# Load order, a weight transposed by DMA, and the first FFN units in token halves: one change to a fused attention and FFN kernel

## The chip, the cores and the metric

The kernel runs on one core of a Trainium2 chip, in one launch. The metric is the device time in microseconds (us), the median of the runs shown; the profile is one execution of its own, with every time counted from the start of its span. PE is the matrix engine (TensorE), DVE is VectorE, ACT is ScalarE, POOL is GpSimd, SP is SyncE, which here only issues DMAs.

## The reference

Two branches work on the same layer-normalised input and are added to it. Everything is bfloat16 in memory; B is 1, S is 2048 tokens, D is 512, there are 32 heads of 16, and F is 1792.

```python
xn = layernorm(A_x)
# branch A: linear attention with a softmax feature map
q, k, v = split(xn @ A_wqkv)                          # heads of 16
pq, pk = q @ w_phi[h], k @ w_phi[h]                   # 16x16 for each head
phi(p) = concat(softmax(p), softmax(-p))              # over the 16 features
kv, z = sum_s phi(pk) v, sum_s phi(pk)
o = (phi(pq) @ kv) / (phi(pq) . z + 1e-6)
# branch B: a bilinear gated FFN
y = ((xn @ w_gate) * (xn @ w_up)) @ w_down
out = A_x + o @ A_wo + y
```

## The kernel before

**Tiles.** Tokens go in 16 tiles of 128 (`n`), and four tiles make a group `T` of 512. `xall` holds x with tokens on the partitions, `xnT` the normalised x transposed, so that D lies on the partitions in four chunks `c`. Token p of tile n is row 16p + n of x: a load of several tiles finds their rows side by side.

**Weights folded.** q and k are never formed. `make_bd` (L212) spreads `w_phi` into a block diagonal `bd`, and `fold` (L225) multiplies it with the transposed wq or wk (`wT2`), which gives `W1q` and `W1k`, four 128x512 blocks in two calls of two blocks each. `features` (L238) then is one projection, two exponentials, a sum, a reciprocal and a product. wk is transposed on PE (`wk_transposes`, L217, two blocks of eight 128x128 transposes, each followed by a ScalarE copy of 128x1024), wq by a transposing DMA (L379) in the middle of the kernel.

**LayerNorm.** The first four tiles go one by one: DVE takes the statistics (L146), aggregates them, adds epsilon, POOL raises to -0.5 (L157), DVE scales (L162), PE transposes (`lt`, L207), ACT copies into `xnT` (L208). DVE runs its instructions in the order in which the code emits them; the statistics of tile n+1 stand ahead of the scaling of tile n. Later groups (`ln_block`) are cut into "chores" that are called between other work; their transposes are DMAs issued on SP.

**FFN.** A unit is one pair (T, f): four matmuls of gate and four of up into two PSUM banks, a ScalarE copy of the gate product (L279), and a DVE product (L280) into `hT`. `ffn(k)` (L263) does the next k units of a list of 56; `fin` (L282) forms the output of a tile from 14 chunks of `hT` and 4 of the attention result.

**Order.** The order on every engine is the order of the code. All matmul results share one pool of six PSUM banks in turn. The first part, and what follows it:

```python
lt(0)
warm_up(2)
vproj(0, amid=lambda: lt(1))
vproj(1, copy=nc.vector.tensor_copy, amid=lambda: lt(2))
wk_transposes(0)
vproj(2, copy=nc.vector.tensor_copy, amid=lambda: lt(3))
wk_transposes(1)
vproj(3, copy=nc.vector.tensor_copy)
ffn(1); fold(1, W1k, (0, 1)); ffn(1); fold(1, W1k, (2, 3)); ffn(1)
```

`vproj(n)` (L310) is four matmuls with wv; after the first two it lets the next tile's transposes in. Ahead of all this PE runs ten warm-up matmuls on zeros. After it come `ln_block(4)`, the k projections of tiles 0 to 3 with units between them, then a loop over tiles 4 to 15 (v, k, unit, kv, unit), and last the attention and `fin` of all tiles with the units that are left.

**Loads.** All loads are issued at the start. SP issues x in pieces (tile 0, tile 1, tiles 2 and 3), wk, the first 256 columns of gate and up, w_phi, columns 256 to 895 of both, x of tiles 4 to 7, the remaining columns, x of tiles 8 to 15, w_down and wo, in that order (L76 to L89). ScalarE issues wv (L97) right after its first activation.

Of the kernel before, what the change touches and what calls it, by code (L numbers as in the profile page):

```python
# [8 lines left out]
BF16 = mybir.dt.bfloat16  # L9
F32 = mybir.dt.float32  # L10
AF = mybir.ActivationFunctionType
ALU = mybir.AluOpType
# [9 lines left out]
def kernel(  # L22
# [12 lines left out]
    nc = tc.nc  # L35
    P = 128
    S, D = A_x.shape[-2], A_x.shape[-1]
    F = B_w_gate.shape[-1]
    H = 32
    DH = D // H  # L40
    NT = S // P
# [5 lines left out]
    TT = GT * P  # L47
    E1 = DH + 1

    x_view = A_x.flatten_outer_dims().rearrange("(p n) d -> p n d", n=NT)  # L50
    out_view = out.flatten_outer_dims().rearrange("(p n) d -> p n d", n=NT)

    consts = ctx.enter_context(tc.tile_pool(name="consts", bufs=1))
    wpool = ctx.enter_context(tc.tile_pool(name="wpool", bufs=1))
# [8 lines left out]
    wo = wpool.tile([P, DC, D], BF16)  # L63

    hpool = ctx.enter_context(tc.tile_pool(name="hpool", bufs=3))
    wk = hpool.tile([P, DC, D], BF16, name="wk", tag="h")
    wT2 = hpool.tile([P, 2, DC, D], BF16, name="wT2", tag="h")

    def dma_x(lo, hi):
        nc.sync.dma_start(out=xall[:, lo:hi, :], in_=x_view[:, lo:hi, :])  # L70

    def dma_cols(eng, w, src, lo, hi, at=0):
        eng.dma_start(out=w[:, :, lo - at:hi - at], in_=src[:, lo:hi].rearrange("(c p) f -> p c f", p=P))

    F1, F2 = 2 * P, 7 * P
    for lo, hi in ((0, 1), (1, 2), (2, 4)):  # L76
        dma_x(lo, hi)
    dma_cols(nc.sync, wk, A_wqkv, D, 2 * D, at=D)
    dma_cols(nc.sync, wg, B_w_gate, 0, F1)
    dma_cols(nc.sync, wu, B_w_up, 0, F1)  # L80
    nc.sync.dma_start(out=wphi[:], in_=A_w_phi.rearrange("(c h) d f -> (h d) c f", c=DC))
    dma_cols(nc.sync, wg, B_w_gate, F1, F2)
    dma_cols(nc.sync, wu, B_w_up, F1, F2)
    dma_x(4, 8)
    dma_cols(nc.sync, wg, B_w_gate, F2, F)
    dma_cols(nc.sync, wu, B_w_up, F2, F)
    dma_x(8, NT)
    nc.sync.dma_start(out=wd[:], in_=B_w_down.rearrange("(c p) d -> p c d", p=P))
    nc.sync.dma_start(out=wo[:], in_=A_wo.rearrange("(c p) n -> p c n", p=P))  # L89
# [4 lines left out]
    nc.vector.memset(zeros[:], 0.0)  # L94
    first = consts.tile([P, 1], BF16)
    nc.scalar.activation(out=first[:], in_=zeros[:, 0:1], func=AF.Exp, scale=1.0)
    dma_cols(nc.scalar, wv, A_wqkv, 2 * D, 3 * D, at=2 * D)  # L97
    ident = consts.tile([P, P], BF16)
    make_identity(nc, ident[:])
    mhalf = consts.tile([P, GT], F32)  # L100
# [38 lines left out]
    def bank(name, dt=F32, n=TT):  # L139
        return ps_s.tile([P, n], dt, name=name, tag="s")  # L140
# [9 lines left out]
        stats = ln_sums(n)  # L150
        nc.vector.bn_aggr(out=mv, in_=stats[:])

    def ln_rstd(mv, k):
        ve = lnpool.tile([P, GT], F32, name="ve")
        nc.vector.tensor_scalar(out=ve[:, 0:k], in0=mv[:, 0:k, 1], scalar1=EPS, scalar2=None, op0=ALU.add)
        rstd = lnpool.tile([P, GT], F32, name="rstd", bufs=GT)
        nc.gpsimd.tensor_tensor(out=rstd[:, 0:k], in0=ve[:, 0:k], in1=mhalf[:, 0:k], op=ALU.pow)  # L157
        return rstd
# [18 lines left out]
    def ln_block(lo):  # L177
        mv = mv_tile()
        nb = lnpool.tile([P, GT], F32, name="nb", bufs=GT)
        rstd = []  # L180

        def scales():
            ve = lnpool.tile([P, GT], F32, name="ve4")
            nc.gpsimd.tensor_scalar(out=ve[:], in0=mv[:, :, 1], scalar1=EPS, scalar2=None, op0=ALU.add)
            r = lnpool.tile([P, GT], F32, name="rstd4", bufs=GT)
            nc.gpsimd.tensor_tensor(out=r[:], in0=ve[:], in1=mhalf[:], op=ALU.pow)
            nm = lnpool.tile([P, GT], F32, name="nm")
            nc.gpsimd.tensor_scalar(out=nm[:], in0=mv[:, :, 0], scalar1=-1.0, scalar2=None, op0=ALU.mult)
            nc.gpsimd.tensor_tensor(out=nb[:], in0=nm[:], in1=r[:], op=ALU.mult)
            rstd.append(r)  # L190

        def apply(i):
            xn = xnpool.tile([P, D], BF16, name="xn")
            nc.scalar.activation(out=xn[:], in_=xall[:, lo + i, :], func=AF.Identity,
                                 scale=rstd[0][:, i:i + 1], bias=nb[:, i:i + 1])
            nc.sync.dma_start(out=xnT[:, :, (lo + i) * P:(lo + i + 1) * P], in_=xn[:], transpose=True)

        for i in range(GT):
            chores.append(lambda i=i: ln_stats(lo + i, mv[:, i, :]))
        chores.append(scales)  # L200
        for i in range(GT):
            chores.append(lambda i=i: apply(i))

    def lt(n):
        tp = bank("tp", BF16).rearrange("p (c t) -> p c t", c=DC)
        for c in range(DC):
            nc.tensor.transpose(out=tp[:, c, :], in_=xns[n][:, c * P:(c + 1) * P], identity=ident[:])  # L207
        nc.scalar.copy(out=xnT[:, :, n * P:(n + 1) * P], in_=tp)  # L208

    bd = consts.tile([P, DC, 8, DH], BF16)  # L210

    def make_bd():  # L212
        bo, wp = BO[:], wphi[:]
        nc.gpsimd.tensor_tensor(out=bd[:], in0=_bcast_ap(bo, [bo.ap[0], [0, DC], [E1, 8], [1, DH]]),
                                in1=_bcast_ap(wp, [wp.ap[0], [DH, DC], [0, 8], [1, DH]]), op=ALU.mult)

    def wk_transposes(jp):  # L217
        tp = bank("tp", BF16, 2 * TT).rearrange("p (c t) -> p c t", c=DC)
        for i in range(2):
            j = jp * 2 + i  # L220
            for c in range(DC):
                nc.tensor.transpose(out=tp[:, c, i * P:(i + 1) * P], in_=wk[:, j, c * P:(c + 1) * P], identity=ident[:])  # L222
        nc.scalar.copy(out=wT2[:, 1, :, jp * 2 * P:(jp + 1) * 2 * P], in_=tp)

    def fold(qk, dst, js, copy=nc.scalar.copy):  # L225
        for j in js:
# [33 lines left out]
    hTs = {}  # L260
    units = [(T, f) for T in range(NGRP) for f in range(FC)]

    def ffn(k):  # L263
        for _ in range(k):
            if not units:
                return
            T, f = units.pop(0)
            if f == 0:
                hTs[T] = hpool.tile([P, FC, TT], BF16, name="hT", tag="h")
            gps = bank("g")  # L270
            for c in range(DC):
                nc.tensor.matmul(gps, lhsT=wg[:, c, f * P:(f + 1) * P], rhs=xnT[:, c, T * TT:(T + 1) * TT],  # L272
                                 start=(c == 0), stop=(c == DC - 1))
            ups = bank("u")
            for c in range(DC):
                nc.tensor.matmul(ups, lhsT=wu[:, c, f * P:(f + 1) * P], rhs=xnT[:, c, T * TT:(T + 1) * TT],  # L276
                                 start=(c == 0), stop=(c == DC - 1))
            g_sb = gpool.tile([P, TT], BF16, name="g_sb")
            nc.scalar.copy(out=g_sb[:], in_=gps)  # L279
            nc.vector.tensor_tensor(out=hTs[T][:, f, :], in0=ups, in1=g_sb[:], op=ALU.mult)  # L280

    def fin(n, parts=1):  # L282
        T, t4 = n // GT, n % GT
        w = D // parts
        for lo in range(0, D, w):
            ps = bank("fin")[:, 0:w]
            for f in range(FC):
                nc.tensor.matmul(ps, lhsT=hTs[T][:, f, t4 * P:(t4 + 1) * P], rhs=wd[:, f, lo:lo + w],  # L288
                                 start=(f == 0), stop=False)
            for c in range(DC):  # L290
                nc.tensor.matmul(ps, lhsT=oTs[n][:, c, :], rhs=wo[:, c, lo:lo + w],  # L291
                                 start=False, stop=(c == DC - 1))
            o_sb = opool.tile([P, w], BF16, name=f"o_sb{w}")
            nc.vector.tensor_tensor(out=o_sb[:], in0=ps, in1=xall[:, n, lo:lo + w], op=ALU.add)  # L294
            nc.sync.dma_start(out=out_view[:, n, lo:lo + w], in_=o_sb[:])


    warm = bank("warm")
# [1 line left out]
    def warm_up(k):  # L300
        for _ in range(k):
            nc.tensor.matmul(warm, lhsT=zeros[:, 0:P], rhs=zeros[:], start=True, stop=True)
# [3 lines left out]
    with tc.tile_pool(name="ps_k", bufs=1, space=PSUM) as ps_k:  # L306
# [3 lines left out]
        def vproj(n, copy=nc.scalar.copy, amid=None):  # L310
            ps = bank("pv")
            proj(ps, n, wv, range(2))
            if amid is not None:
                amid()
            proj(ps, n, wv, range(2, DC))
            copy(out=vts[n % NV][:, :, :, 0:DH], in_=ps.rearrange("p (a b c) -> p a b c", a=8, b=4))  # L316
# [17 lines left out]
        for n in range(GT):  # L334
            stats = ln_sums(n)
            if n > 0:
                first_apply(n - 1)
            nc.vector.bn_aggr(out=mvs[n][:, 0, :], in_=stats[:])
            rstds.append(ln_rstd(mvs[n], 1))
        first_apply(GT - 1)  # L340
        make_bd()
        nc.gpsimd.tensor_tensor(out=M4[:], in0=BO[:, 0:4, :], in1=BO[:, 4:8, :], op=ALU.add)
        lt(0)
        warm_up(2)
        vproj(0, amid=lambda: lt(1))
        vproj(1, copy=nc.vector.tensor_copy, amid=lambda: lt(2))
        wk_transposes(0)
        vproj(2, copy=nc.vector.tensor_copy, amid=lambda: lt(3))
        wk_transposes(1)
        vproj(3, copy=nc.vector.tensor_copy)  # L350
        ffn(1)
        fold(1, W1k, (0, 1))
        ffn(1)
        fold(1, W1k, (2, 3))
        ffn(1)
        ln_block(4)
        ffn(1)
        chore(2)
# [16 lines left out]
        chore()  # L375
        ffn(1)
        kv(1)
        ffn(1)
        nc.sync.dma_start(out=wT2[:, 0, :, :], in_=A_wqkv[:, 0:D], transpose=True)  # L379
        for n in range(GT, NT):  # L380
            if n in (4, 8):
# [87 lines left out]
```

## Time and profile before

| | |
|---|---|
| median of 3 runs | 225.45 us (225.12 to 225.52) |
| the profiled execution | 224.9 us, of which its span is 223.2 us |
| PE busy | 217.4 us, 97% of the span |
| DVE, ACT, POOL busy | 137.9, 90.3, 72.1 us |
| read from HBM, written | 9.19 MB, 2.10 MB |

The page divides the span into 40 slices of 5.6 us and gives for each the busy share of an engine in tenths. The chain of waits follows the work that ended last back to the start; a piece of it gives its start, its duration, the engine and the line. A duration of a matmul includes the drain of its pipeline, so that four matmuls of 512 columns in a row show 0.86 us when others follow, and about 0.17 more when PE waits after them. For a DMA the view gives the time of issue and the time from there to its landing.

### The profile page before, as it was taken

Reading aid. Unit: us, or ns where it says so; the run is one execution under the profiler, and the core shown is the slowest. Engines: PE = TensorE matmul, PEld = TensorE weight load, DVE = VectorE, ACT = ScalarE, POOL = GpSimd, SP = SyncE. Lnnn points to the kernel's source line nnn. Section 1 sums busy time; section 2 is a strip of 40 time slices with the busy share of each in tenths; the row PEclk is TensorE's granted clock in tenths of the full one; section 3 lists DMA queues with packets and bytes.
Section 4 is the critical chain, followed back from the end, with each engine's and each line's share of the span. In section 5 each row is a group of like instructions: output and inputs, shape, how many; then the busy total and the mean of one; then the engine's idle time right before and its main releaser. Section 6 shows DMA issues by size and latency. Waiting matters only on the chain.

```text
span 223.2 us, 3437 instructions
## 1 busy us (share of the span) xinstructions
PE 217.4 (97%) x1278; PEld 105.4 (47%) x1278; DVE 137.9 (62%) x237; ACT 90.3 (40%) x161; POOL 72.1 (32%) x59
## 2 busy tenths in 40 slices
PE   7799999999999999999999999999999999999994
PEld 2354444445444444444454444444444444444453
DVE  5634986586559875757679975097745746444321
ACT  2574575448955685646354122222222222100000
POOL 3310455336235663636315453014033033000000
PEclk9999999999999999999999999999999999999999
DMA  6999923501110224020203664314431431622301
GB/s 178 317 381 394 349 55 74 94 1 21 38 38 0 47 50 94 1 47 3 47 1 71 99 140 94 75 24 94 94 73 24 93 72 24 91 55 71 72 25 47
DMA packets 44481, 19.91 MB, mean 89 GB/s; under 512 B 35248, under 2 KB 44080, under 8 KB 44336
## 3 DMA queue, kind: packets, MB, share of 16 engines
q1 hardware_dynamic: 43936, 19.16, 34.8%
q10 hardware_dynamic: 528, 0.52, 0.8%
q8 instruction: 10, 0.16, 0.3%
q14 instruction: 7, 0.06, 0.1%
HBM read 9.19 MB, written 2.10 MB: 51 GB/s over the span
## 4 chain that ended last, share of the span: by engine, by line
PE 95%; DMA 2%; DVE 1%; SPq 0%; ACT 0%; issue 0%
PE fin L288 22%; PE u L276 22%; PE g L272 22%; PE fin L291 6%; PE k L235 6%; PE q L235 6%; PE pv L235 6%; DMA xall<-in_A_x_dram 2%; PE ab L412 2%; PE kv L324 2%; PE pq L229 1%; PE tp L222 0%; PE tp L207 0%; SPq L70 0%; DVE stats L146 0%; ACT xnT L208 0%
## 5 line engine op out<-in xcount | busy, mean ns | idle before, releaser
L276 PE MATMUL u<-xnT,wu 128*128 128x512 bf16 x224 | 57.5, 379 | 0.0
L272 PE MATMUL g<-xnT,wg 128*128 128x512 bf16 x224 | 57.5, 379 | 0.0
L280 DVE TENSOR_TENSOR hT<-u,g_sb 128x512 bf16<-128x512 f32 x56 | 37.1, 668 | 28.3 <-PE u L276 19.5
L247 DVE TENSOR_REDUCE sums<-e 128x64 f32<-128x1024 f32 x32 | 38.9, 1215 | 21.5 <-ACT e L244 21.5
L279 ACT CAST g_sb<-g 128x512 bf16<-128x512 f32 x56 | 32.9, 588 | 46.5 <-PE g L272 46.5
L288 PE MATMUL fin<-wd,hT 128*128 128x512 bf16 (+1 forms) x238 | 51.1, 366 | 0.0
L251 POOL TENSOR_TENSOR phiq<-e,rs 128x1024 bf16<-128x1024 f32 x16 | 30.9, 1932 | 61.5 <-DVE rs L249 53.2
L251 POOL TENSOR_TENSOR phik<-e,rs 128x1024 bf16<-128x1024 f32 x16 | 30.9, 1932 | 47.6 <-DVE rs L249 45.6
L276 PEld LDWEIGHTS <-wu 128*128 128x128 bf16 x224 | 21.9, 98 | 26.4
L288 PEld LDWEIGHTS <-hT 128*128 128x128 bf16 x238 | 23.0, 98 | 24.1
L272 PEld LDWEIGHTS <-wg 128*128 128x128 bf16 x224 | 21.1, 98 | 23.4
L235 PEld LDWEIGHTS <-xnT 128*128 128x128 bf16 x192 | 17.2, 97 | 18.7 <-ACT xnT L208 1.7
L294 DVE TENSOR_TENSOR o_sb<-fin,xall 128x512 bf16<-128x512 f32 (+1 forms) x17 | 11.2, 656 | 22.4 <-PE fin L291 22.4
L243 ACT ACTIVATE e<-q 128x512 f32<-128x512 f32 x16 | 9.5, 596 | 26.1 <-PE q L235 26.1
L249 DVE RECIPROCAL rs<-sums 128x64 f32<-128x64 f32 x32 | 17.7, 553 | 3.1
L235 PE MATMUL pv<-wv,xnT 128*128 128x512 bf16 x64 | 16.9, 379 | 0.6 <-ACT xnT L208 0.5
L291 PE MATMUL fin<-wo,oT 128*128 128x512 bf16 (+1 forms) x68 | 16.6, 366 | 0.0
L235 PE MATMUL k<-W1k,xnT 128*128 128x512 bf16 x64 | 16.4, 379 | 0.0
L235 PE MATMUL q<-W1q,xnT 128*128 128x512 bf16 x64 | 16.4, 378 | 0.0
L243 ACT ACTIVATE e<-k 128x512 f32<-128x512 f32 x16 | 9.6, 597 | 7.0 <-PE k L235 7.0
L316 ACT CAST vt<-pv 128x512 bf16<-128x512 f32 x13 | 7.7, 591 | 11.5 <-PE pv L235 11.5
L146 DVE BATCH_NORM_STATS2 stats<-xall 128x6 f32<-128x512 bf16 x16 | 10.7, 670 | 2.2 <-DMA xall<-in_A_x_dram 2.2
(50 smaller groups left out, 125.1 us busy)
## 6 DMA issues: line engine op xcount, KB each, us to landing
out_dram<-o_sb SPq DMA_DIRECT2D x15, 128.0 KB, 1.9
wd<-in_B_w_down_dram SPq DMA_DIRECT2D x1, 1792.0 KB, 17.5
xall<-in_A_x_dram SPq DMA_DIRECT2D x1, 1024.0 KB, 13.4
wg<-in_B_w_gate_dram SPq DMA_DIRECT2D x1, 896.0 KB, 8.5
wu<-in_B_w_up_dram SPq DMA_DIRECT2D x1, 896.0 KB, 11.4
wg<-in_B_w_gate_dram SPq DMA_DIRECT2D x1, 640.0 KB, 7.9
wu<-in_B_w_up_dram SPq DMA_DIRECT2D x1, 640.0 KB, 7.0
wv<-in_A_wqkv_dram ACTq DMA_DIRECT2D x1, 512.0 KB, 4.4
```

The costliest lines, as they stand in the source:

```text
L235: nc.tensor.matmul(ps, lhsT=xnT[:, j, n * P:(n + 1) * P], rhs=w[:, j, :], start=(j == 0), stop=(j == DC - 1))
L243: nc.scalar.activation(out=e[:, :, 0, :], in_=pfv, func=AF.Exp, scale=1.0)
L247: nc.vector.tensor_reduce(out=sums[:], in_=ev, axis=AX.X, op=ALU.add)
L249: nc.vector.reciprocal(out=rs[:].rearrange("p a b -> p (a b)"), in_=sums[:])
L251: nc.gpsimd.tensor_tensor(out=phi[:].rearrange("p g (x f) -> p (g x) f", f=DH), in0=ev, in1=rs[:].to_broadcast((P, 2 * H, DH)), op=ALU.mult)
L272: nc.tensor.matmul(gps, lhsT=wg[:, c, f * P:(f + 1) * P], rhs=xnT[:, c, T * TT:(T + 1) * TT], start=(c == 0), stop=(c == DC - 1))
L276: nc.tensor.matmul(ups, lhsT=wu[:, c, f * P:(f + 1) * P], rhs=xnT[:, c, T * TT:(T + 1) * TT], start=(c == 0), stop=(c == DC - 1))
L279: nc.scalar.copy(out=g_sb[:], in_=gps)
L280: nc.vector.tensor_tensor(out=hTs[T][:, f, :], in0=ups, in1=g_sb[:], op=ALU.mult)
L288: nc.tensor.matmul(ps, lhsT=hTs[T][:, f, t4 * P:(t4 + 1) * P], rhs=wd[:, f, lo:lo + w], start=(f == 0), stop=False)
L291: nc.tensor.matmul(ps, lhsT=oTs[n][:, c, :], rhs=wo[:, c, lo:lo + w], start=False, stop=(c == DC - 1))
L294: nc.vector.tensor_tensor(out=o_sb[:], in0=ps, in1=xall[:, n, lo:lo + w], op=ALU.add)
```

## The change

The loads are all issued on SP, in a new order: x of tile 0, tile 1, tiles 2 and 3, then wv, the first 256 columns of gate and up, w_phi, columns 256 to 511, then wk as a transposing DMA from DRAM straight into `wT2`, columns 512 to 1151, x of tiles 4 to 7, and the rest. wk's plain load, its sixteen PE transposes and their two copies are gone. Token p of tile n in the first group is now row 128n + p; the other twelve tiles have rows 512 + 12p + (n - 4). The copies of the first two transposed tiles are made in two halves, one warm-up fewer is run, v1's copy goes from DVE to ScalarE, and the first two FFN units are done for tokens 0 to 255 between the v projections and for tokens 256 to 511 after them. One unit that stood before `vproj(4)` now comes ahead of the first k projection. `ln_rstd` takes the engine as an argument, with the same instructions on the same engines as before.

```diff
-    x_view = A_x.flatten_outer_dims().rearrange("(p n) d -> p n d", n=NT)
-    out_view = out.flatten_outer_dims().rearrange("(p n) d -> p n d", n=NT)
+    def token_views(ap):
+        rows = ap.flatten_outer_dims()
+        first = rows[0:TT, :].rearrange("(n p) d -> p n d", p=P)
+        rest = rows[TT:S, :].rearrange("(p n) d -> p n d", p=P)
+        return lambda lo, hi: first[:, lo:hi, :] if hi <= GT else rest[:, lo - GT:hi - GT, :]
...
-    F1, F2 = 2 * P, 7 * P
-    for lo, hi in ((0, 1), (1, 2), (2, 4)):
-        dma_x(lo, hi)
-    dma_cols(nc.sync, wk, A_wqkv, D, 2 * D, at=D)
-    dma_cols(nc.sync, wg, B_w_gate, 0, F1)
-    dma_cols(nc.sync, wu, B_w_up, 0, F1)
+    def dma_gu(lo, hi):
+        dma_cols(nc.sync, wg, B_w_gate, lo * P, hi * P)
+        dma_cols(nc.sync, wu, B_w_up, lo * P, hi * P)
+
+    dma_x(0, 1)
+    dma_x(1, 2)
+    dma_x(2, 4)
+    dma_cols(nc.sync, wv, A_wqkv, 2 * D, 3 * D, at=2 * D)
+    dma_gu(0, 2)
     nc.sync.dma_start(out=wphi[:], in_=A_w_phi.rearrange("(c h) d f -> (h d) c f", c=DC))
-    dma_cols(nc.sync, wg, B_w_gate, F1, F2)
-    dma_cols(nc.sync, wu, B_w_up, F1, F2)
+    dma_gu(2, 4)
+    nc.sync.dma_start(out=wT2[:, 1, :, :], in_=A_wqkv[:, D:2 * D], transpose=True)
+    dma_gu(4, 9)
     dma_x(4, 8)
-    dma_cols(nc.sync, wg, B_w_gate, F2, F)
-    dma_cols(nc.sync, wu, B_w_up, F2, F)
+    dma_gu(9, FC)
     dma_x(8, NT)
...
-    dma_cols(nc.scalar, wv, A_wqkv, 2 * D, 3 * D, at=2 * D)
...
-    def lt(n):
+    def lt(n, parts=1):
...
-        nc.scalar.copy(out=xnT[:, :, n * P:(n + 1) * P], in_=tp)
+        for c in range(0, DC, DC // parts):
+            nc.scalar.copy(out=xnT[:, c:c + DC // parts, n * P:(n + 1) * P], in_=tp[:, c:c + DC // parts, :])
...
-    def wk_transposes(jp):
...
+    def unit(T, f, lo=0, hi=TT):
+        if T not in hTs:
+            hTs[T] = hpool.tile([P, FC, TT], BF16, name="hT", tag="h")
+        pss = []
+        for w, name in ((wg, "g"), (wu, "u")):
+            ps = bank(name)[:, 0:hi - lo]
+            for c in range(DC):
+                nc.tensor.matmul(ps, lhsT=w[:, c, f * P:(f + 1) * P], rhs=xnT[:, c, T * TT + lo:T * TT + hi],
+                                 start=(c == 0), stop=(c == DC - 1))
+            pss.append(ps)
+        g_sb = gpool.tile([P, TT], BF16, name="g_sb")
+        nc.scalar.copy(out=g_sb[:, 0:hi - lo], in_=pss[0])
+        nc.vector.tensor_tensor(out=hTs[T][:, f, lo:hi], in0=pss[1], in1=g_sb[:, 0:hi - lo], op=ALU.mult)
...
-        lt(0)
-        warm_up(2)
-        vproj(0, amid=lambda: lt(1))
-        vproj(1, copy=nc.vector.tensor_copy, amid=lambda: lt(2))
-        wk_transposes(0)
+        lt(0, parts=2)
+        warm_up(1)
+        vproj(0, amid=lambda: lt(1, parts=2))
+        vproj(1, amid=lambda: lt(2))
+        unit(0, 0, 0, 2 * P)
         vproj(2, copy=nc.vector.tensor_copy, amid=lambda: lt(3))
-        wk_transposes(1)
+        unit(0, 1, 0, 2 * P)
         vproj(3, copy=nc.vector.tensor_copy)
+        for f in range(2):
+            unit(0, f, 2 * P, TT)
+        del units[0:2]
         ffn(1)
         fold(1, W1k, (0, 1))
         ffn(1)
         fold(1, W1k, (2, 3))
-        ffn(1)
         ln_block(4)
...
         kv(1)
-        ffn(1)
         nc.sync.dma_start(out=wT2[:, 0, :, :], in_=A_wqkv[:, 0:D], transpose=True)
```

More of the change, by code (lines that the diff above doesn't have):

```diff
@@ L48 @@
     E1 = DH + 1
-    x_view = A_x.flatten_outer_dims().rearrange("(p n) d -> p n d", n=NT)
-    out_view = out.flatten_outer_dims().rearrange("(p n) d -> p n d", n=NT)
+    def token_views(ap):
[3 more added lines that the diff above has]
+        return lambda lo, hi: first[:, lo:hi, :] if hi <= GT else rest[:, lo - GT:hi - GT, :]
+    x_view = token_views(A_x)
+    out_view = token_views(out)
     consts = ctx.enter_context(tc.tile_pool(name="consts", bufs=1))
@@ L65 @@
     hpool = ctx.enter_context(tc.tile_pool(name="hpool", bufs=3))
-    wk = hpool.tile([P, DC, D], BF16, name="wk", tag="h")
     wT2 = hpool.tile([P, 2, DC, D], BF16, name="wT2", tag="h")
     def dma_x(lo, hi):
-        nc.sync.dma_start(out=xall[:, lo:hi, :], in_=x_view[:, lo:hi, :])
+        nc.sync.dma_start(out=xall[:, lo:hi, :], in_=x_view(lo, hi))
     def dma_cols(eng, w, src, lo, hi, at=0):
         eng.dma_start(out=w[:, :, lo - at:hi - at], in_=src[:, lo:hi].rearrange("(c p) f -> p c f", p=P))
-    F1, F2 = 2 * P, 7 * P
-    for lo, hi in ((0, 1), (1, 2), (2, 4)):
-        dma_x(lo, hi)
-    dma_cols(nc.sync, wk, A_wqkv, D, 2 * D, at=D)
-    dma_cols(nc.sync, wg, B_w_gate, 0, F1)
-    dma_cols(nc.sync, wu, B_w_up, 0, F1)
+    def dma_gu(lo, hi):
[6 more added lines that the diff above has]
+    dma_gu(0, 2)
     nc.sync.dma_start(out=wphi[:], in_=A_w_phi.rearrange("(c h) d f -> (h d) c f", c=DC))
-    dma_cols(nc.sync, wg, B_w_gate, F1, F2)
-    dma_cols(nc.sync, wu, B_w_up, F1, F2)
+    dma_gu(2, 4)
+    nc.sync.dma_start(out=wT2[:, 1, :, :], in_=A_wqkv[:, D:2 * D], transpose=True)
+    dma_gu(4, 9)
     dma_x(4, 8)
-    dma_cols(nc.sync, wg, B_w_gate, F2, F)
-    dma_cols(nc.sync, wu, B_w_up, F2, F)
+    dma_gu(9, FC)
     dma_x(8, NT)
@@ L151, in ln_stats, with ln_rstd @@
         nc.vector.bn_aggr(out=mv, in_=stats[:])
-    def ln_rstd(mv, k):
+    def ln_rstd(eng, mv, k):
         ve = lnpool.tile([P, GT], F32, name="ve")
-        nc.vector.tensor_scalar(out=ve[:, 0:k], in0=mv[:, 0:k, 1], scalar1=EPS, scalar2=None, op0=ALU.add)
+        eng.tensor_scalar(out=ve[:, 0:k], in0=mv[:, 0:k, 1], scalar1=EPS, scalar2=None, op0=ALU.add)
         rstd = lnpool.tile([P, GT], F32, name="rstd", bufs=GT)
@@ L182, in scales @@
         def scales():
[L183 to L186, printed above, removed]
+            r = ln_rstd(nc.gpsimd, mv, GT)
             nm = lnpool.tile([P, GT], F32, name="nm")
@@ L215, in make_bd @@
                                 in1=_bcast_ap(wp, [wp.ap[0], [DH, DC], [0, 8], [1, DH]]), op=ALU.mult)
-    def wk_transposes(jp):
[L218 to L223, printed above, removed]
     def fold(qk, dst, js, copy=nc.scalar.copy):
@@ L261 @@
     units = [(T, f) for T in range(NGRP) for f in range(FC)]
+    def unit(T, f, lo=0, hi=TT):
[11 more added lines that the diff above has]
+        nc.vector.tensor_tensor(out=hTs[T][:, f, lo:hi], in0=pss[1], in1=g_sb[:, 0:hi - lo], op=ALU.mult)
     def ffn(k):
         for _ in range(k):
[L265 to L280, printed above, removed]
+            if units:
+                unit(*units.pop(0))
     def fin(n, parts=1):
@@ L294, in fin @@
             nc.vector.tensor_tensor(out=o_sb[:], in0=ps, in1=xall[:, n, lo:lo + w], op=ALU.add)
-            nc.sync.dma_start(out=out_view[:, n, lo:lo + w], in_=o_sb[:])
+            nc.sync.dma_start(out=out_view(n, n + 1)[:, 0, lo:lo + w], in_=o_sb[:])
     warm = bank("warm")
@@ L338 @@
             nc.vector.bn_aggr(out=mvs[n][:, 0, :], in_=stats[:])
-            rstds.append(ln_rstd(mvs[n], 1))
+            rstds.append(ln_rstd(nc.vector, mvs[n], 1))
         first_apply(GT - 1)
```

## The prediction

> **What bounds the kernel now.** I read the page first: busy time by engine, the slices, the chain that ended last.
>
> ```profile
> span 223.2 us, 3437 instructions
> PE 217.4 (97%) x1278; PEld 105.4 (47%) x1278; DVE 137.9 (62%) x237; ACT 90.3 (40%) x161; POOL 72.1 (32%) x59
> PE   7799999999999999999999999999999999999994
> DMA  6999923501110224020203664314431431622301
> PE 95%; DMA 2%; DVE 1%; SPq 0%; ACT 0%; issue 0%
> ```
>
> PE is the chain. It is full from the third slice to the last one (a slice is 5.6 us), so time can be won in two ways only: by fewer PE instructions, or by closing PE's idle time in the first 12 us, where the page also shows full DMA engines. So the second view is the chain of waits, cut to 5 to 13 us (columns: start us, duration us, what).
>
> ```profile
> 1.71 4.88 DMA xall<-in_A_x_dram
> 6.61 0.69 DVE stats L146
> 7.31 0.33 DVE xn L162
> 7.68 0.41 PE tp L207 x4
> 8.11 0.59 ACT xnT L208
> 8.75 0.60 PE pv L235 x2
> 10.01 0.45 PE tp L222 x8
> 11.55 0.46 PE tp L222 x8
> 12.05 1.04 PE pv L235 x4
> ```
>
> The start hangs on the x load for tiles 2 and 3, issued at 1.71 and landed at 6.59, although only 512 KB of x is wanted by then. LayerNorm statistics of tile 2 wait for it, DVE is in order, so the scaling of tile 1 (7.31), its transposes (7.68), its copy (8.11) and the second v projection (8.75) all follow. Two blocks of eight wk transposes (L222) then lie on the chain itself. The same chain up to 22 us shows the first k projection at 20.89, after four FFN units (g and u, 0.86 each) and two folds (0.45 each).
>
> Why is that x load late? The DMA view, cut to 3.2 to 4.5 us (queue: packets, MB, share of the engines), and two stretches of the windows view (last columns: DMA share, GB/s):
>
> ```profile
> q10 hardware_dynamic: 352, 0.36, 100.6%
> q1 hardware_dynamic: 3, 0.00, 0.3%
> 10.00:12.00 2.00, 1.99 (x25) 1.34 (x22) 1.35 (x3) 1.70 (x3) 1.22 (x2) 1.00 1.07 360
> 39.40:42.20 2.80, 2.80 (x21) 1.37 (x20) 0.66 (x2) 2.15 (x4) 0.70 (x1) 1.00 1.09 187
> ```
>
> q10 is wv, the one load that ScalarE issues. For these 1.3 us it has all sixteen engines, and the x load, already issued on SyncE (q1), moves nothing.
>
> **The change, part by part.** I follow the chain's own times.
>
> *wv behind x on SyncE (gain 1.1 to 1.2 us).* x for tiles 2 and 3 no longer stands behind 512 KB of wv, so it should land near 4.6 (the earlier x loads take 2.3 us from issue; it is twice their size). DVE then goes from tile 1 (ve ends at 5.5) straight to the statistics of tile 2, at 5.5 instead of 6.61: 1.1 earlier, and the scaling of tile 1 ends at 6.5 instead of 7.63. The Trainium skill ("DMA: Bandwidth & Descriptors", section "Issuing engines are not separate DMA queues") says that DMAs from different engines interleave on the same engines, and that a second issuer saves only sequencer time. By that rule x would have shared the engines and landed about 5.2 (an estimate), the wait would not exist and this term would be near 0. The rows above show one queue having everything, so I keep 1.1.
>
> *Price of it: wv lands later.* No row shows wv in that place. It is bounded by its own landing before, 1.22 + 4.4 = 5.6, and by that of wk, which stood behind x and wv: 2.18 + 6.3 = 8.5. x and wv are 1.05 MB; the windows move 22 KB up to 2 us, then 224, 235 and 330 GB/s per microsecond to 5, then 284, which makes 1.05 MB at 5.85. A landing trails the last packet by about 0.3 (wv landed at 5.6, its queue is silent after 5.3), so I take 6.3, near what PE waits for anyway: xnT of tile 0 let the first v projection start at 6.33. Then: first half of v0 at 6.33, transposes of tile 1 at 6.76, their copy. The copy is now two halves; ScalarE's 512-element copy takes 587 ns and the 1024-element one 1012, so 256 elements should take about 375. Half the copy ends at 7.5 and v1 starts near **7.55 instead of 8.75: 1.2 us**. From wv = 6.3 on, each microsecond later costs one.
>
> *wk by DMA transpose (gain 0.9 + 0.2).* Sixteen transposes leave PE: 0.45 + 0.45 on the chain. Their two 1012 ns copies leave ScalarE; the second runs ahead of nothing needed, but the first delays the copy of tile 3 (11.41), which makes v3 wait and pay its drain again: about 0.2 goes.
>
> *Price of it: the transposing load.* It stands in the SyncE queue behind x, wv, the first two pairs of gate and up columns, and w_phi. It replaces the plain wk load, so bytes ahead fall by 512 KB for the first gate and up columns: before they landed at 2.65 + 6.7 = 9.35 and 3.2 + 7.2 = 10.4; at 360 GB/s they now come 1.45 earlier, 7.9 and 8.95. w_phi (10.7 before) comes at 9.25, the next 512 KB of gate and up at 10.7. The same transposing load, for q, moved its 512 KB at 39.4 to 42.2 on an otherwise idle queue: 2.8 us, 187 GB/s. Bounds under load: 1.45 (a plain load's rate) and 9.6 (four xnT transposes of 128 KB, 2.4 us each from issue to landing). I take 2.8, since it is the same tile, shape and source: landed at 13.5. The fold wants it when units 0 to 2 are done, at 16.05 (sum below): 2.5 us of cover. Behind it on the queue stand the gate and up columns 4 to 8 (1.31 MB, 3.55 us, at 17.0; wanted by unit 4 at 18.7 and 19.55) and x for tiles 4 to 7 (18.5; DVE wants it after unit 4's product, 21.2). All three have about 2.5 us of cover, so they fail together. The wd and wo loads end some 1.4 us later; the first xnT transpose waits for ScalarE at 30.07, landed 2.5 us later, and v4 is read near 38, so this is hidden.
>
> *Token halves, two units moved forward (cost 0.05).* Units 0 and 1 as 32 matmuls of 256 columns instead of 16 of 512: the last output group's 14 matmuls of 256 take 1.53 us (109 ns each) and 14 of 512 take 3.02 (216), so 16 pairs cost 16 x 2.9 ns. Their gate columns are wanted at 8.8 and up columns at 9.25: covers of 0.9 and 0.3, each late microsecond counts. ScalarE, in order: v0's copy to 8.5, tile 2 to 9.1, v1 (moved there from DVE, 0.59) to 9.7, half product to 10.1, tile 3 from 10.4 to 11.0; v3 starts at 11.5, so 0.5 of cover. DVE is lighter by one 0.69 copy. One warm-up fewer (0.22) lay in the wait for xnT: nothing.
>
> *Later moves.* One unit moves from behind the second k/v product to before the first k projection. DVE is 8.79 us busy of 10 between 20 and 30, but the stretch from the first k projection on has the same order, and starts 0.5 earlier with one unit more done. Contiguous token tiles change rows, not bytes; the last output store stays in the second view: nothing.
>
> *Sum.* From v1 at 7.55: v1 half with drain 0.60, tile 2 0.22, v1 0.43, half unit 0.88, v2 half 0.43, tile 3 0.22, v2 0.43, half unit 0.88, v3 0.86, two half units 1.76, unit 2 1.73 = 16.0; fold 0.45, unit 3 1.73, fold 0.45 = 18.65. Before, the same work (four units, two folds) ended at 20.89. **Gain 2.2 us** (1.2 + 0.9 + 0.2, less 0.05). The profiled execution takes 224.9 (span 223.2 and 1.7 around it) and becomes 222.7; the median of 225.45 lies 0.55 above it, so I predict 223.2.
>
> **The rivals.** *Transposing load too slow, slower than before.* If the transposing traffic among plain loads goes at the pace of the single xnT rows (9.6 us), wk lands at 20.3, the fold waits 4.3, and with the 2.2 won the time is 227.5. It decides from 7.6 us on (landing at 18.3). For: even alone it moved half the plain rate, in packets that the DMA view puts under 512 B. Against: the 2.8 us row is the same load. 0.10.
> *wv late.* At 7.4, halfway to wk's landing, v1 starts at 8.6 and the gain is 1.15: 224.3. For: the early windows move only 224 to 235 GB/s. Against: x leaves the same 1.05 MB in front that the windows had carried by 5.85. 0.20.
> *No change.* wv as late as 8.5 leaves a gain of 0.1 (225.3): 0.06.
>
> **How the numbers follow.** Forecast 0.64, the rivals 0.20, 0.06 and 0.10. The limit of about 0.2% (0.45 us) is what a measurement here can tell from no change. The two first cases are faster: 0.84. Range: wv at 6.1 starts v1 at 7.4 and wins 2.35 (223.1); the fastest run lay 0.33 below the median, and v1's drain of 0.17 may go too, so the low end is 222.5. At the other end wv at 7.9 starts v1 at 9.1 and leaves 0.65, 224.8, which takes in most of that case.
>
> **What would show it.** Right: the x wait of DVE at tile 2 gone, no L222 rows, v1 near 7.55, first k projection at 20.4 with five units done, PE full after 9. Wrong: PE at the first fold or unit 4 waiting for the transposing load or wg and wu, DVE waiting for x tiles 4 to 7, or the first v projection waiting for wv beyond 6.5.

## The result and the profile after

The changed kernel takes 222.69 us (222.54 to 222.90, 4 runs) where the kernel before took 225.37 beside it: a ratio of 0.9883, interval 0.9866 to 0.9900, 2.7 us less. The profiled execution went from 224.9 to 222.54. The same kernel, run again beside experiments, gave 222.84 against 225.09 (0.9897, interval 0.9883 to 0.9911), 2.25 us less. The forecast was 223.2, 2.25 under the 225.45 it started from; whether the first set's 2.7 is more than scatter these runs do not tell. A few runs of e4, e6 and e10 took 1 to 2 us longer than the others of the same kernel: the ratios take them in, and the times given are medians.

The page of the changed kernel, in the lines that answer to those shown of before:

```profile
span 220.8 us, 3448 instructions
PE 216.0 (98%) x1277; PEld 106.1 (48%) x1277; DVE 138.3 (63%) x238; ACT 89.3 (40%) x164; POOL 72.3 (33%) x59
PE   7899999999999999999999999999999999999994
DMA  6999964402201223020204944314431431722311
PE 96%; DMA 2%; SPq 1%; DVE 0%; issue 0%
```

PE is 1.4 us less busy, and by these tenths only the second slice (5.5 to 11 us) is fuller than it was. The chain of waits, cut to the first 24 us (L232 is the projections, L211 the transposes, L226 the fold; the code has moved):

```profile
2.18 4.26 DMA wv<-in_A_wqkv_dram
6.48 0.59 PE pv L232 x2
7.76 0.61 PE pv L232 x2
11.86 0.86 PE pv L232 x4
16.19 0.45 PE pq L226 x8
20.54 0.86 PE k L232 x4
```

The chain no longer goes through x, DVE and two blocks of wk transposes: it goes through wv, for which PE waits 0.7 us (waits view: us in total, times, longest):

```profile
PE pv L232 <- DMA wv<-in_A_wqkv_dram: 0.7, 1, 0.7
```

v1 starts at 7.76 (before 8.75), the first fold at 16.19, and the first k projection at 20.54 with five units done (before 20.89 with four): 0.35 + 1.73 = 2.08 us won by then, and 2.14 at the last matmul, so nearly all of it was won ahead of the first k projection. The remaining 0.26 of the profile's 2.4 lies in the last output store, whose end trails DVE's last product by 2.36 us where it was 2.62. In the other twelve profiles of this study it trails by 2.38 to 2.54, with old rows as with new, so this part is taken for scatter. From v1 on the waits view lists no wait of PE.

Two rows of the DMA view (last column: us from issue to landing, a median; the second row holds the loads of wk and of wq, 5.8 for wk's alone), and the transposing load's own line in SyncE's timeline:

```profile
xall<-in_A_x_dram SPq DMA_DIRECT2D x1, 256.0 KB, 3.0
wT<-in_A_wqkv_dram SPq DMA_TRANSPOSE x2, 5.8
```

```profile
6.28 3.85 SPq L91 DMA_TRANSPOSE wT<-in_A_wqkv_dram  x1
```

x of tiles 2 and 3 landed at 1.71 + 3.0 = 4.7. wk was issued at 6.28, held SyncE for 3.85 us and landed at 12.1, 4.1 us before the fold wanted it.

### The profile page after: what moved, and what is told of

Its sections match the earlier page's. It is cut to its first block, busy times and chain, and to the rows that moved or that the text cites. A ratio compares the mean times of both kernels' runs of the same rounds, so it can differ in the third digit from the quotient of the medians.

```text
span 220.8 us, 3448 instructions
## 1 busy us (share of the span) xinstructions
PE 216.0 (98%) x1277; PEld 106.1 (48%) x1277; DVE 138.3 (63%) x238; ACT 89.3 (40%) x164; POOL 72.3 (33%) x59
## 4 chain that ended last, share of the span: by engine, by line
PE 96%; DMA 2%; SPq 1%; DVE 0%; issue 0%
PE fin L285 22%; PE u L267 22%; PE g L267 22%; PE pv L232 6%; PE fin L288 6%; PE q L232 6%; PE k L232 6%; DMA wv<-in_A_wqkv_dram 2%; PE ab L410 2%; PE kv L321 2%; PE pq L226 1%; SPq L75 1%; PE tp L211 0%; DVE o_sb L291 0%
## 5 line engine op out<-in xcount | busy, mean ns | idle before, releaser
L267 PE MATMUL u<-xnT,wu 128*128 128x512 bf16 (+1 forms) x232 | 57.8, 372 | 0.0
L267 PE MATMUL g<-xnT,wg 128*128 128x512 bf16 (+1 forms) x232 | 57.8, 372 | 0.0
L272 DVE TENSOR_TENSOR hT<-u,g_sb 128x512 bf16<-128x512 f32 (+1 forms) x58 | 37.4, 649 | 28.2 <-PE u L267 19.3
L271 ACT CAST g_sb<-g 128x512 bf16<-128x512 f32 (+1 forms) x58 | 33.3, 574 | 46.9 <-PE g L267 46.9
L267 PEld LDWEIGHTS <-wu 128*128 128x128 bf16 x232 | 22.7, 98 | 25.7
L267 PEld LDWEIGHTS <-wg 128*128 128x128 bf16 x232 | 22.0, 98 | 23.3
L232 PEld LDWEIGHTS <-xnT 128*128 128x128 bf16 x192 | 17.3, 97 | 18.3 <-ACT xnT L213 1.1
L232 PE MATMUL pv<-wv,xnT 128*128 128x512 bf16 x64 | 16.9, 379 | 0.7 <-DMA wv<-in_A_wqkv_dram 0.7
L232 PE MATMUL k<-W1k,xnT 128*128 128x512 bf16 x64 | 16.4, 379 | 0.0
L232 PE MATMUL q<-W1q,xnT 128*128 128x512 bf16 x64 | 16.4, 378 | 0.0
L313 ACT CAST vt<-pv 128x512 bf16<-128x512 f32 x14 | 8.3, 592 | 10.9 <-PE pv L232 10.9
L419 DVE TENSOR_TENSOR otok<-ab,rden 128x512 bf16<-128x512 f32 x16 | 11.1, 691 | 0.6
```

Source lines behind the costliest of these rows:

```text
L232: nc.tensor.matmul(ps, lhsT=xnT[:, j, n * P:(n + 1) * P], rhs=w[:, j, :], start=(j == 0), stop=(j == DC - 1))
L267: nc.tensor.matmul(ps, lhsT=w[:, c, f * P:(f + 1) * P], rhs=xnT[:, c, T * TT + lo:T * TT + hi], start=(c == 0), stop=(c == DC - 1))
L271: nc.scalar.copy(out=g_sb[:, 0:hi - lo], in_=pss[0])
L272: nc.vector.tensor_tensor(out=hTs[T][:, f, lo:hi], in0=pss[1], in1=g_sb[:, 0:hi - lo], op=ALU.mult)
L419: nc.vector.tensor_tensor(out=o_tok[:].rearrange("p (b h d) -> p b h d", b=2, d=DH), in0=abv[:, :, :, 0:DH], in1=rden[:].to_broadcast((P, ...
```

## The experiments

Each is a few lines away from the changed kernel or from the kernel before. They ran in three sets (e1 to e4; e6, e8, e9; e5, e10 to e12), each beside the kernel before, which took 225.05, 225.09 and 225.07 us. The changed kernel ran in the second set, 222.84 us; "above" a time means above that. "PE end" compares the last matmul in the profiles of the experiment and of the changed kernel in that second set. Some starts in that profile, ahead of the values of the profile shown above: wv landed at 6.36, v0 at 6.40, v1 at 7.68, first fold at 16.11, first k projection at 20.46.

**Units whole (e1).** Nothing between the v projections:

```diff
-        unit(0, 0, 0, 2 * P)
...
-        unit(0, 1, 0, 2 * P)
...
-        for f in range(2):
-            unit(0, f, 2 * P, TT)
-        del units[0:2]
-        ffn(1)
+        ffn(3)
```

> The changed kernel with units 0 and 1 done whole, for all 512 tokens, after the four v projections (nothing between them); all else as changed. Theory A (the halves are cover): with the wk transposes gone, PE has nothing to do while tile 3 goes through LayerNorm (its scaling ends at 10.0), its transposes and its copy; v3 starts near 11.1 with v0 to v2 done, unit 2 ends near 17.2 instead of 16.2, time about 1.0 us above the changed kernel (223.7). Theory B (the prediction's sum, where the halves only cost 0.05 us): the time stays within 0.1 us of the changed kernel's 222.7.

223.79 us (ratio 0.9942, interval 0.9930 to 0.9954), 0.95 above the changed kernel. The chain of this run:

```profile
8.94 0.59 ACT xnT L213
9.58 0.61 PE pv L232 x2
10.50 0.59 ACT xnT L213
11.14 1.04 PE pv L232 x4
```

PE waits for ScalarE's copies of tiles 2 and 3: v3 starts at 11.14, as theory A had it. This execution had already begun late, with v1 at 8.07, because its warm-up ran longer (see e8). So the better measure is from v1 to the first k projection, which is free of that: 13.63 us here (8.07 to 21.70), 12.78 in the changed kernel, a difference of 0.85. The halves are cover for LayerNorm, not an extra of 0.05 us.

**wv on ScalarE (e2).** The load goes back to where it was issued before:

```diff
-    dma_cols(nc.sync, wv, A_wqkv, 2 * D, 3 * D, at=2 * D)
...
+    dma_cols(nc.scalar, wv, A_wqkv, 2 * D, 3 * D, at=2 * D)
```

> The changed kernel with wv issued by ScalarE at the place it had before; all else as changed. Theory A (prediction): wv goes ahead of x for tiles 2 and 3, that load lands near 6.5 again, the second v projection starts near 8.75 instead of 7.76, time 1.0 us above the changed kernel (223.7). Theory B (loads of two issuers interleave packet by packet, so the issuer does not matter): x lands by about 5.2, DVE does not wait for it, time within 0.2 us of the changed kernel's 222.7.

223.59 (0.9936, 0.9924 to 0.9948), 0.75 above; PE end 1.03 later. The chain again begins with the x load:

```profile
1.71 4.84 DMA xall<-in_A_x_dram
6.57 0.69 DVE stats L153
7.63 0.40 PE tp L211 x4
```

x landed at 6.55, not 5.2: theory A. From 3.2 to 4.5 us the DMA view gives wv's queue (ScalarE, issued at 1.22) 77.3% of the engines and SyncE's queue, with x issued at 1.71, 9.8%; in the kernel before it was 100.6% and 0.3%. The load that was issued first was served first for the most part, though in e2 not alone.

**wk transposed on PE (e3).**

```diff
-    nc.sync.dma_start(out=wT2[:, 1, :, :], in_=A_wqkv[:, D:2 * D], transpose=True)
+    dma_cols(nc.sync, wk, A_wqkv, D, 2 * D, at=D)
...
         del units[0:2]
+        wk_transposes(0)
         ffn(1)
+        wk_transposes(1)
```

> The changed kernel with wk loaded plainly at the same place of the queue and transposed on PE in two blocks of eight, after the second token halves and after unit 2, each with its copy; all else as changed. Theory A (prediction): sixteen transposes at 56 ns put 0.9 us back on PE, which is full there; time 0.9 us above the changed kernel (223.6), x for tiles 4 to 7 lands about 1 us earlier. Theory B (the transposing load itself cost PE something, by late weights): less than 0.5 us above.

223.70 (0.9939, 0.9926 to 0.9952), 0.86 above: theory A. (Its PE end is 1.57 later, of which 0.53 is wv, landed at 6.89 in that execution and at 6.36 in the changed kernel.)

**wk further back (e4, e5).** The transposing load moved behind x of tiles 4 to 7, then behind all gate and up columns. The diff is e4's; in e5 the added line stands after `dma_gu(9, FC)`.

```diff
-    nc.sync.dma_start(out=wT2[:, 1, :, :], in_=A_wqkv[:, D:2 * D], transpose=True)
     dma_gu(4, 9)
     dma_x(4, 8)
+    nc.sync.dma_start(out=wT2[:, 1, :, :], in_=A_wqkv[:, D:2 * D], transpose=True)
     dma_gu(9, FC)
```

> The changed kernel with the transposing load of wk moved behind the gate and up columns 512 to 1151 and x of tiles 4 to 7. Theory A (one queue, in order of issue): 1.83 MB more stand ahead of it, about 5 us at 360 GB/s, so it lands near 17.1 where the first fold wants it at 16.2; PE waits 0.9 us there, time 0.9 us above the changed kernel (223.6). Theory B (a transposing load does not queue behind the plain loads): it lands near 12 to 13 as it did, no wait, 222.7.

> The changed kernel with the transposing load of wk moved still further back, behind all gate and up columns. Theory A (one queue in order, PE waits for what is late beyond 16.2): another 1.31 MB, 3.5 us, lands it near 20.6, the first fold waits 4.4 us, time 4.4 us above the changed kernel (227.2), slower than the kernel before. Theory B (the other loads, now earlier, free work that fills the wait): no later than 1.5 us above.

e4 takes 223.82 (0.9962, 0.9945 to 0.9979), 1.0 above by the medians and 1.5 by the ratios; wk lands at 17.15 and the wait is the expected one. e5 takes 229.39 (1.0191, 1.0178 to 1.0204), slower than the kernel before. The waits view of e4, then of e5 (engine, line, waited for: us in total, times, longest):

```profile
PE pq L226 <- DMA wT<-in_A_wqkv_dram: 0.9, 1, 0.9
```

```profile
PE pq L226 <- DMA wT<-in_A_wqkv_dram: 4.2, 1, 4.2
```

The landing (20.8) and the wait of e5 were as theory A had them, but the time is 6.5 above, not 4.4. The windows view of e5 says why (PEclk stands ahead of the last two columns):

```profile
18.00:20.00 2.00, 0.00 (x0) 0.00 (x0) 0.00 (x0) 0.00 (x0) 0.00 (x0) 1.00 1.27 253
20.00:22.00 2.00, 1.13 (x9) 0.96 (x10) 0.00 (x0) 0.51 (x2) 0.00 (x0) 0.73 0.96 204
22.00:24.00 2.00, 2.00 (x6) 0.76 (x5) 0.00 (x0) 0.94 (x3) 0.00 (x0) 0.50 0.95 379
24.00:26.00 2.00, 2.00 (x16) 1.08 (x14) 0.69 (x1) 1.06 (x3) 0.00 (x0) 0.91 1.10 383
```

After 4.2 us without work the granted clock fell to 0.50 and came back in the stretch from 24 us on: the chain of e5 has a fold at 1.01 where it takes 0.45, the gate matmuls after it at 1.71 and the up matmuls at 1.30 where each takes 0.86: 1.85 us on top of the wait. (In a finer windows view the clock is at 0.50 from 21.4 to 24.0 and at 1.00 from 24.4.) The first fold starts at 20.87, 4.76 later than in the changed kernel, and 4.76 + 1.85 = 6.61 is the delay at PE's end, 6.62. The 0.9 us wait of e4 left the clock at 1.00. The Trainium skill's "TensorE: Matmul & The Clock Gate" (section "Part 1: The HAM clock gate") puts the fall to half at an idle window of about 3.4 us and the return at about as long a busy one; both runs agree with it.

**Rows of before (e6).** The old token map, for x and the output; wv stays on SyncE.

```diff
-    x_view = token_views(A_x)
-    out_view = token_views(out)
+    x_rows = A_x.flatten_outer_dims().rearrange("(p n) d -> p n d", n=NT)
+    out_rows = out.flatten_outer_dims().rearrange("(p n) d -> p n d", n=NT)
```

> The changed kernel with the token map of before (row 16p + n) for x and the output. Theory A (prediction: the map changes rows, not bytes): within 0.1 us of the changed kernel. Theory B (the rows of one tile side by side load faster): x of tile 0 lands 0.1 to 0.3 us later and tiles 2 and 3 as much, wv with them, time 0.1 to 0.5 us above.

223.78 (0.9947, 0.9928 to 0.9967), 0.94 above; PE end 1.07 later, all of it before v0: tile 0's statistics start at 3.69 (changed: 2.97), and wv lands at 7.42 (6.36):

```profile
2.17 5.25 DMA wv<-in_A_wqkv_dram
7.47 0.59 PE pv L232 x2
```

Theory B, and more than it had. So I crossed rows and issuer.

**Rows and issuer crossed (e10, e11, e12).** e10 is the kernel before with wv issued by SyncE behind x; e11 is that with the new rows as well; e12 is the changed kernel with both undone. The diff is e10's, from the kernel before.

```diff
     for lo, hi in ((0, 1), (1, 2), (2, 4)):
         dma_x(lo, hi)
+    dma_cols(nc.sync, wv, A_wqkv, 2 * D, 3 * D, at=2 * D)
...
-    dma_cols(nc.scalar, wv, A_wqkv, 2 * D, 3 * D, at=2 * D)
```

> The kernel before with one edit: wv is issued by SyncE behind x of tiles 2 and 3 (rows, wk, units as before). Theory A (after the run with the old rows: without another load between them the strided x loads land late, tile 0 at 3.6 instead of 2.99): tile 0 loses what tile 2 wins, v1 starts near 8.7 as before, time within 0.3 us of the kernel before. Theory B (the prediction's term: the order alone wins 1.0 to 1.2 us): 224.0.

> The kernel before with two edits: wv issued by SyncE behind x of tiles 2 and 3, and the first 512 tokens in contiguous tiles; wk, its PE transposes and the units as before. Theory A (rows and order win together): tile 0 lands at 2.9, tiles 2 and 3 by 4.8, v1 starts near 7.9 (the copy of tile 1 is whole here), time 0.8 to 1.0 us under the kernel before. Theory B (without the other parts the won time turns into waiting for wk or for tile 3): less than 0.4 us under.

> The changed kernel with both load edits undone: rows as before and wv issued by ScalarE. Theory A (the rows matter only where the x loads stand directly behind one another): the start is that of the run with wv on ScalarE and new rows, v1 near 8.5 to 8.75, time 0.8 to 1.0 us above the changed kernel. Theory B (the rows cost 1.0 us wherever wv is): 1.8 to 2.0 us above it.

| kernel | rows | wv issued by | time, us | ratio, interval |
|---|---|---|---|---|
| before | old | ScalarE | 225.07 | |
| e10 | old | SyncE | 225.13 | 1.0005, 0.9990 to 1.0019 |
| e11 | new | SyncE | 224.22 | 0.9961, 0.9948 to 0.9973 |
| e12 (changed, loads undone) | old | ScalarE | 223.77 | 0.9934, 0.9922 to 0.9946 |
| e2 | new | ScalarE | 223.59 | 0.9936, 0.9924 to 0.9948 |
| e6 | old | SyncE | 223.78 | 0.9947, 0.9928 to 0.9967 |
| changed | new | SyncE | 222.84 | 0.9897, 0.9883 to 0.9911 |

From e12, new rows alone win 0.18 us, which the intervals do not tell from nothing, and SyncE alone nothing; both together win 0.93. From the kernel before, SyncE alone wins nothing and both win 0.85 (the new rows alone were not run there). e10 has theory A's time by another route: in its profiled execution (226.07, 0.9 above its median) tile 0 landed at 3.07, but wv only at 8.39. In e11 v1 started at 8.08 and in e12, behind the late x, at 8.77: theory A both times. The windows view from 3 to 5 us, of the changed kernel, e6 and e10 (last column: GB/s):

```profile
3.00:5.00 2.00, 2.00 (x7) 0.63 (x5) 1.83 (x5) 0.00 (x0) 0.58 (x1) 1.00 0.96 252
```

```profile
3.00:5.00 2.00, 2.00 (x7) 0.62 (x5) 1.24 (x4) 0.00 (x0) 0.12 (x1) 1.00 0.84 201
```

```profile
3.00:5.00 2.00, 2.00 (x6) 0.67 (x5) 1.76 (x5) 0.00 (x0) 0.58 (x1) 1.00 0.82 160
```

With the old rows and everything in one queue, the first 512 KB of x and what follows move at 160 and 201 GB/s while the DMA share stays above 0.8: the engines are busy and deliver less. These are two executions, and the 160 is of the one that took 226.07; the nine profiles with new rows and wv on SyncE have 227 to 272. Why rows 16 KB apart are slower, and why little of it shows when ScalarE's load runs beside them, these runs do not tell.

**wv in two loads (e8), and the POOL product later as well (e9).** The first diff is in both, the second in e9 alone.

```diff
-    dma_cols(nc.sync, wv, A_wqkv, 2 * D, 3 * D, at=2 * D)
+    for c in range(0, DC, 2):
+        nc.sync.dma_start(out=wv[:, c:c + 2, :], in_=wv_rows[:, c:c + 2, :])
```

```diff
+        nc.gpsimd.tensor_tensor(out=M4[:], in0=BO[:, 0:4, :], in1=BO[:, 4:8, :], op=ALU.add)
         make_bd()
-        nc.gpsimd.tensor_tensor(out=M4[:], in0=BO[:, 0:4, :], in1=BO[:, 4:8, :], op=ALU.add)
```

> The changed kernel with wv loaded in two halves (D chunks 0 and 1, then 2 and 3), one behind the other at the same place. Theory A (the start now hangs on wv alone: PE waits 0.7 us for it, xnT is ready at 6.0 and the tile 1 scaling at 6.5): the first half lands by 5.9, v0 starts near 6.05 instead of 6.48, v1 near 7.4 instead of 7.76, time 0.35 to 0.4 us under the changed kernel. Theory B (a landing has a fixed part, so half the bytes come hardly sooner, or the chain through tile 3 takes the gain back): less than 0.15 us under.

> As the kernel with wv in halves, and POOL forms the block diagonal of w_phi after the small mask instead of before it. In the changed kernel the DVE scaling of tile 3 took 1.24 us beside that POOL product, and 0.41 without it. Theory A (the two slow each other): the scaling of tile 3 is done by 9.3 instead of 10.0, and with wv in halves, where tile 3 is wanted at 9.9, another 0.1 us is won. Theory B (DVE was waiting for something else there): the scaling stays long, no gain over wv in halves.

e8 takes 222.77 (0.9891, 0.9878 to 0.9904) and e9 222.83 (0.9895, 0.9883 to 0.9908): no gain over 222.84. PE no longer waits for wv in their profiles, but v0 starts at 6.58, because the warm-up and the transposes of tile 0 ran longer. The timeline of the changed kernel and of e8:

```profile
1.24 3.92 PE L299 MATMUL warm<-zeros 128*128 128x512 bf16 x10 [1.24 <-DVE zeros L102]
```

```profile
1.24 4.45 PE L301 MATMUL warm<-zeros 128*128 128x512 bf16 x10 [1.24 <-DVE zeros L104]
```

The same ten matmuls take 3.82 to 4.09 us in six of the fourteen profiles of this study and 4.37 to 4.45 in eight, with the granted clock at 1.00 throughout. Each profile is one execution, and a few tenths between two profiles can come from this alone. In e8's the longer warm-up hides what the earlier wv could give; whether it gives anything otherwise stays open, and the timed runs say it is under what they can tell. e9 settles the other question only in part: the scaling of tile 3 took 0.41 us with the POOL product out of its way. So it did in e8, where w_phi came later and moved the product as well.

## Why the prediction was right, and where it was not

**The path.** Right within 0.21 us at each of these points: no wait of DVE for tiles 2 and 3 (landed 4.7, predicted 4.6), tile 1 scaled at 6.47 (6.5), wv at 6.44 (6.3), v1 at 7.76 (7.55), first fold at 16.19 (16.05), first k projection at 20.54 (20.4), statistics of tile 4 on DVE at 21.25 (21.2). The sum of 2.2 was 2.14 at PE's end. The largest miss, v1, came from v0, which began 0.15 late and whose first half shows 0.59 where the working counts 0.43. With v0 at 6.48, wv stopped just short of the 6.5 that was to be a sign of being wrong.

**The issuer.** The row was kept against the Trainium skill's rule ("DMA: Bandwidth & Descriptors", section "Issuing engines are not separate DMA queues"), and e2 agrees with the row more than with the rule (77.3% against 9.8%): it brings the late x back, and 0.75 us with it. But the term needs the rows, see below.

**The transposing load.** Priced at 2.8 us on the wire and 13.5 landed; it landed at 12.1 with 4.1 us of cover instead of 2.5. Behind the other loads it was no slower than alone: from 9.5 to 11.5 us the DMA view shows 0.52 MB at 260 GB/s, nearly all in packets under 512 B, where the load for q took 2.8 us at 187. x of tiles 4 to 7 landed at 19.65, later than the 18.5 predicted. SyncE issued it only at 11.35, behind the 3.85 us that the transposing issue held the queue; but in the changed kernel's second profile it was issued at 11.27 and landed at 17.97, so the late issue does not explain it, and these runs do not tell what does. Its cover sufficed: no wait of PE follows.

**The terms that were mis-sized, two.** First the wk term: 0.9 + 0.2 were written to removing the transposes, and the token halves went in as a cost of 0.05. From e11 (new loads, wk on PE) to e1 (wk by DMA, no halves) the time falls by 0.43 only; from e1 to the changed kernel the halves give 0.95. The 0.43 takes in more than the transposes, since e1 also has tile 1's copy in halves, one warm-up fewer and v1's copy on ScalarE, which were not run alone. From v1 to the first k projection, with five units done, e11 takes 13.87 us (12.14 and a fifth unit at 1.73), e1 13.63 and the changed kernel 12.78: 0.24 for the transposes, 0.85 for the halves. The two together are 1.09, close to the 0.9 + 0.2 - 0.05 of the prediction, but the split was wrong. In the start of the kernel before, the transposes stood in time that PE otherwise spends waiting for tile 3; taking them out makes that a wait, and the halves fill it. The sum came out since it counted PE's work as if it were always full, which the halves made true. (With the halves in place wk on PE costs 0.86, by e3.) Second, "contiguous token tiles: nothing" was wrong: it is 0.94 us with wv on SyncE (e6), and without it the wv estimate of 6.3 would have been 7.4. That estimate used the bytes that the windows of before had moved, with ScalarE's load beside the x loads; the same bytes in one queue with the old rows take 1 us longer. The predicted landing held by luck, through an edit that the prediction had set aside.

**The slow rival.** The slow pace that it gave as its reason was not seen (260 GB/s, above). A late wk at the first fold, put there by position, does cross over to slower than before (e5), yet the rival's price was a straight microsecond for each microsecond late. That holds roughly for 0.9 us (e4, 1.0 by the medians), and not for 4.2 us, which cost 6.5.

## What to carry to other kernels

When PE is the bound, count what is taken off it only where PE was not about to wait anyway: look at what is late next, and put independent work there in the same edit. A load order, a row map and the queue that issues them are one design; testing each alone here would have rejected both. And a wait of PE long enough to lower its clock is paid again after it ends, here by 1.85 us after a wait of 4.2.

## What the runs showed of the hardware

- x in rows of 1 KB that lie 16 KB apart, followed in the same queue by wv: 160 and 201 GB/s from 3 to 5 us (two executions), against 227 to 272 with rows side by side (nine).
- A 512 KB transposing load held SyncE's queue for 3.85 us behind other loads, for 6.52 and 8.97 with more of them ahead (e4, e5), and for 2.30 us in the middle of the kernel before. The load behind it was issued only after that, at 10.18 in the changed kernel.
- A DVE scaling that starts within 0.1 us of a POOL product ends after it and takes three times as long, while the product takes 1.08 us with it and without it. In the changed kernel the scaling of tile 3 starts just ahead of the POOL product:

```profile
8.77 1.24 DVE L169 TENSOR_SCALAR xn<-xall,mv,rstd 128x512 bf16<-128x512 bf16 x1 [0.67 <-POOL rstd L164]
```

```profile
8.79 1.08 POOL L219 TENSOR_TENSOR bd<-BO,wphi 128x512 bf16<-128x512 bf16 x1
```

```profile
8.81 0.41 DVE L171 TENSOR_SCALAR xn<-xall,mv,rstd 128x512 bf16<-128x512 bf16 x1 [0.66 <-POOL rstd L166]
```

The third line is e9's. The skill's "SBUF — State Buffer" (section "SBUF: two separate sides") describes a port pair that the two engines take whole, one after the other; 8.79 + 1.08 = 9.87 for POOL's end and 10.01 for DVE's fit that, though by the profile's starts DVE was there first by 0.02 us. In the changed kernel's second profile POOL was first by 0.07 (1.16 for DVE, ends at 9.85 and 10.00); in e6, where DVE was 0.24 ahead, it took its 0.41. It cost nothing here, since tile 3's transposes were wanted about then anyway.
